# Negated-sine plane, full-row narrow matmuls, a moved radix trick and a new order in an S4 + gated-MLP kernel

## Chip, cores, metric

One core of a Trainium2 chip. The metric is device time in microseconds (us) of one launch. Before the change: 361.38 us, the median of three runs (360.59 to 361.48).

## The reference, cut to what matters

Sequence length L = 2048, width D = 640, state N = 128, MLP width F = 1728, all bf16.

```python
def _A_ref(u, ...):                      # S4: u is the layernorm of x
    logdA = dt * (A_re + 1j * A_im)
    P = exp(logdA[:, :, None] * l)       # table over N and l
    K = einsum("dn,dnl,dn->dl", Cc, P, dB).real
    y = irfft(rfft(pad(u)) * rfft(pad(K)))[:L]
    return y + u * Dskip
h  = x + _A_ref(layernorm(x), ...)
g, up = layernorm(h) @ w_gate, layernorm(h) @ w_up
return h + (sigmoid(g) * up) @ w_down
```

## The kernel before

The kernel K is factored into two tables, A and B, that PE multiplies group by group (`pk`). Picking matmuls gather the lags (`ps_kv`), their spectra are formed (`ps_xk`), and VectorE multiplies them with the spectra of u. The sequence is cut into four blocks of 512 rows; each block b has an inverse transform (`ps_y`), a residual, a LayerNorm and an MLP. Block b's MLP on PE runs beside the spectral products and the inverse of block b + 1.

Table B's steps, one C-tile of 160 columns at a time; the last two lines are the half-size operations:

```python
t   = s * sine_plane(mi)         # both halves (re, im) at once
dst = s * cosine_plane(mi)
V(dst[:, 0], dst[:, 0], t[:, 1], ALU.subtract)
V(dst[:, 1], dst[:, 1], t[:, 0], ALU.add)
```

The narrow matmuls, one contraction row each (cut):

```python
MM(pv[0:32, 0], lhsT=one[64:65, :], rhs=edge[64:65, dc]..., tile_position=(64, 0))          # "one",  32 columns
MM(ps[0:NL, 1, ...], lhsT=last[0:1, q, 0, :], rhs=kv[0:1, 3 + q, ...])                      # "pair", NL = 14 columns
MM(ps[96:128, a, W:2 * W], lhsT=sel[32:33, 0, :], rhs=edge[32:33, ...], tile_position=(32, 96))  # "sel", 32 columns
```

The radix trick for a block in `R4` (12 VectorE operations, half as many inverse matmuls), the transposition of the normalised rows, and the down-projection's residual (cut):

```python
for ft in range(1 if b in R4 else 2): ...        # inverse: 16 or 32 matmuls
# turn(b): DMA if DT[b], else 20 PE transposes, through ml_po's banks if PW, else ml_pg's
po = ... # second half of the down-projection: ml_pg/ml_pu banks if PW, else ml_po's
tb = Wd[:, 15, 320 * c:320 * c + 320]
nc.scalar.copy(tb, po[k][c][:, 0:320])
nc.vector.tensor_tensor(h2[:, c], tb, h2[:, c], ALU.add)
```

The order of instructions comes from a scheduler that reads one priority for each unit of work, in the dictionary `AT`.

Of the kernel before, what the change touches and what calls it, by code (L numbers as in the profile page):

```python
# [8 lines left out]
DT = mybir.dt  # L9
F32, BF16, F16, I32, I16 = DT.float32, DT.bfloat16, DT.float16, DT.int32, DT.int16  # L10
AF = mybir.ActivationFunctionType
ALU = mybir.AluOpType
PSUM = bass.MemoryType.PSUM
PI = math.pi
P = 128
# [7 lines left out]
W = 160  # L23
NC = D // W
UH = 320
EO = (1, 3)
R4 = (2,)
AT = {"eb": -38.3, "ea0": -22.2, "tb0": -12.8, "cb": -5.3, "bb0": 10.0, "st0": -13.2, "ta0": 20.7, "ch0": -25.4, "A0": 1.0, "st1": -127.2,
      "st2": -38.2, "st3": 34.0, "tb1": 45.8, "bb1": 28.9, "n0": -8.7, "ta1": 48.0, "ch1": 54.1, "A1": -23.3, "tb2": 49.0, "bb2": 68.1,
      "ea1": 70.7, "n1": 53.4, "ta2": 71.2, "ch2": 33.5, "A2": 32.8, "tb3": 73.0, "bb3": 75.3, "n2": -7.5, "s0": 66.5, "l0": -14.7,  # L30
      "i0": 94.9, "ta3": -15.7, "ch3": -6.7, "A3": -12.7, "n3": 0.8, "s1": 76.0, "l1": -16.4, "i1": 219.0, "i2": -7.7, "LATER": 49.5,
      "LATER2": 98.7, "EARLY": -11.7, "s2": 58.8, "p0": -14.4, "p1": -3.4, "p2": -13.4, "PW": 1, "w0": 29.5, "w1": -19.5, "w2": 66.8,
      "w3": 82.8, "DT": (0, 0, 0, 0), "NG": (1, 0, 0, 0), "TAIL": -45.1, "NA": (1, 2, 0, 0), "SA": (2, 0, 0, 3),
      "K": (42.3, 65.1, 109.8, 202.7), "F": (-18.0, 64.3, 14.3, 46.5), "G": (2.6, 0.5, 2.3, 0)}

# [7 lines left out]
FIRST = {1: 0, 2: 2, 3: 4}  # L43
M_SHIFT = (0, 1, 2, 8, 9, 10)
B_STEPS = ((1, 2, (0, 1, 1), 2), (2, 4, (0, 2, 1), 1), (4, 8, (0, 4, 1), 0), (8, 12, (0, 4, 1), 3), (12, 16, None, 4),
           (16, 18, (0, 16, 8), 5), (18, 21, (12, 17, 2), 5))


# [5 lines left out]
def host_consts():  # L54
# [38 lines left out]
    for c in range(4):  # L93
        pick[4 * np.arange(32) + c, c, np.arange(32)] = 1.0
    last = np.zeros((P, 3, 4, NL))
    for c in range(4):
        last[c, 0, c, 0:4] = 1.0
        last[c, 1, c, 4:10] = 1.0
        last[c, 2, c, 10:14] = 1.0
    one = np.zeros((P, 32))  # L100
# [7 lines left out]
def bc(ap, shape):  # L108
    return ap.to_broadcast(shape)
# [23 lines left out]
def full_kernel(tc, ins, out):  # L133
# [55 lines left out]
    G = cload(xp, "G", [P, 2, 2, 2, 4, P], tag="G")  # L189
    pick = cload(cp, "pick", [P, 4, 32])  # L190
    last = cload(cp, "last", [P, 3, 4, NL])
    one = cload(cp, "one", [P, 32])
    KM = cload(xp, "KM", [P, 2, 2, 2, NK, P], tag="X")
    sel = cload(cp, "sel", [P, 2, 32])
    cor = cp.tile([P, 40], F32, name="cor")
    xc = cp.tile([P, 40], BF16, name="xc")
    edge = cp.tile([96, D], BF16, name="edge")
    sy.dma_start(edge[64:65, :], ins["A_Dskip"].rearrange("(o d) -> o d", o=1))
    uh = cp.tile([NL, D], BF16, name="uhead")
# [26 lines left out]
    for i in range(2):  # L226
# [3 lines left out]
        nc.vector.scalar_tensor_tensor(fr[:, i, 1], phi, 2.0 ** -19, fr[:, i, 0], ALU.mult, ALU.subtract)  # L230
    mg = tabp.tile([P, 2, P], F16, name="mg")
    ones = tabp.tile([P, 1], F16, name="ones")
    nc.gpsimd.memset(ones[:], 1.0)
    nc.gpsimd.memset(mg[:, 0], MAGIC16 / P)
    nc.gpsimd.memset(mg[:, 1], 0.25 / P)

    def turns(items, o, w):

        ps = ps2.tile([P, 2, 512], F32, name="ps_t", tag="p2")
        m = len(items) // 2  # L240
        for a in range(2):
            MM(ps[:, a, 0:m * w], lhsT=mg[:, 0], rhs=bc(ones[:], [P, m * w]), start=True, stop=False)
            for q in range(m):
                src, dk, oo = items[a * m + q]
                for i in range(2):
                    MM(ps[:, a, q * w:q * w + w], lhsT=dg[:, dk, :], rhs=fr[:, src, i, o + oo:o + oo + w], start=False, stop=(q == m - 1 and i == 1))  # L246
        v = ps[:, :, 0:m * w].bitcast(I16).rearrange("p a (n t) -> p a n t", t=2)[:, :, :, 0]

        def quarter():
            for a in range(2):  # L250
                MM(ps[:, a, 0:m * w], lhsT=mg[:, 1], rhs=bc(ones[:], [P, m * w]), start=False, stop=True, skip_group_check=True)

        return v, quarter
# [5 lines left out]
    rstd = cp.tile([P, 16], F32, name="rstd")  # L259
    st = cp.tile([P, 16, 2, 6], F32, name="ln_st", tag="ln_st")  # L260
    nmr = cp.tile([P, 16], F32, name="nmr")
# [32 lines left out]
    def trig_b(c):  # L294
        M = T["MB", c] = tabp.tile([P, 2, 6, W], BF16, name="tabMB", bufs=2)
        v, quarter = turns([(0, 16, 0), (0, 17, 0), (0, 15, 0), (1, 16, 0), (1, 17, 0), (1, 15, 0)], W * c, W)
        act_fn(TWO(M[:, 1]), v, AF.Sin, scale=SIN_SCALE16)
        quarter()
        act_fn(TWO(M[:, 0]), v, AF.Sin, scale=SIN_SCALE16)

    def bases_b(c):
        M = T["MB", c]
        for ri in range(2):
            V(M[:, ri], EB[:, :, W * c:W * c + W], M[:, ri], ALU.mult)

# [68 lines left out]
    def chain_b(c):  # L374
        X, M = T["B", c], T["MB", c]
        tS = tabp.tile([P, 8 * W], BF16, name="tS")
        for d0, d1, src, mi in B_STEPS:
            n = d1 - d0
            t = tS[:, 0:2 * n * W].rearrange("p (i n w) -> p i n w", i=2, n=n)
            dst = X[:, :, d0:d1, :]  # L380
            if src is None:
                for ri in range(2):
                    s4 = X[:, ri, 0:16, :].rearrange("p (a b) w -> p a b w", a=2)[:, :, 0:2, :]
                    t4, d4 = (v.rearrange("p (a b) w -> p a b w", a=2) for v in (t[:, ri], dst[:, ri]))
                    for o4, pl in ((t4, 1), (d4, 0)):
                        V(o4, s4, bc(M[:, pl:pl + 1, mi:mi + 1, :], [P, 2, 2, W]), ALU.mult)
            else:
                s = X[:, :, slice(*src), :]
                V(t, s, bc(M[:, 1:2, mi:mi + 1, :], [P, 2, n, W]), ALU.mult)
                V(dst, s, bc(M[:, 0:1, mi:mi + 1, :], [P, 2, n, W]), ALU.mult)  # L390
            V(dst[:, 0], dst[:, 0], t[:, 1], ALU.subtract)
            V(dst[:, 1], dst[:, 1], t[:, 0], ALU.add)
# [4 lines left out]
    def ln_stats(st, mv, src, r):  # L397
        for hh in range(2):
            nc.vector.bn_stats(st[:, r, hh, :], src(r)[:, 320 * hh:320 * hh + 320])  # L399
        nc.vector.bn_aggr(mv[:, r, :], st[:, r, :, :].rearrange("p a b -> p (a b)"))  # L400

# [52 lines left out]
    def kmm(c):  # L454
# [16 lines left out]
        def diagonal(g1, kts):  # L471
# [5 lines left out]
            for c4 in range(4):  # L477
                for m in range(4):
                    MM(pv[32 * m:32 * m + 32, :, :, c4], lhsT=pick[:, c4, :], rhs=kj[:, :, :, 4 * m + c4], start=not c4, stop=(m > 0 and c4 == 3), tile_position=(0, 32 * m))  # L479
            MM(pv[0:32, 0], lhsT=one[64:65, :], rhs=edge[64:65, dc].rearrange("p (g c) -> p g c", c=4), start=False, stop=True, tile_position=(64, 0))  # L480
            for c4 in range(4):
                MM(pl[:, :, c4], lhsT=last[:, 2, c4, :], rhs=kts[:, :, 80 + c4], start=not c4, stop=False)
            nc.scalar.copy(kv[:, :, 4 * g1:4 * g1 + 4 * GC], ps[:, 0, 0:20 * GC].rearrange("p (j x) -> p j x", j=5))
            for q in range(2):
                MM(ps[0:NL, 1, 0:4 * GC], lhsT=last[0:1, q, 0, :], rhs=kv[0:1, 3 + q, 4 * g1:4 * g1 + 4 * GC], start=False, stop=(q == 1))
            nc.scalar.copy(edge[0:NL, dc], ps[0:NL, 1, 0:4 * GC])
# [31 lines left out]
    def prod(c, fs):  # L518
# [6 lines left out]
        t2 = prp.tile([P, 2, 2, 2, W], BF16, name="t2", tag="t2", bufs=1)  # L525
        for ft in fs:
            V(t1[:, ft], Z0[:, ft, :, :, o:o + W], S01[:, 0, ft, :, :, o:o + W], ALU.mult)
            V(t2[:, ft], Z0[:, ft, :, :, o:o + W], S01[:, 0, ft, :, ::-1, o:o + W], ALU.mult)
        V(y[:, f, :, 0], t1[:, f, :, 0], t1[:, f, :, 1], ALU.subtract)
# [9 lines left out]
    def inv0(c, fs=((0, 1),), done=None):  # L539
# [6 lines left out]
        for a in range(2):  # L546
            with tc.issue_after(T["mm"]):
                MM(pv[:, a], lhsT=ident[:], rhs=hv[:, a], start=True, stop=False)
            if a:
                MM(ps[96:128, a, W:2 * W], lhsT=sel[32:33, 0, :], rhs=edge[32:33, o:o + W], start=False, stop=False, tile_position=(32, 96))  # L550
        for fg in fs:
# [175 lines left out]
    def edges(psp):  # L727
# [5 lines left out]
        nc.scalar.copy(ct[0:8, :].rearrange("p (q w) -> p q w", q=2), ps[0:8, :, 0:UH])  # L733
        sy.dma_start(dcor[:], ct[0:8, :])
        for b, (t0, t1) in ROWS.items():
            sy.dma_start(xc[16 * FIRST[b]:16 * (FIRST[b] + t1 - t0), :], lanes(x2d[512 * b + 508 + t0:512 * b + 508 + t1, :]))
        sy.dma_start(cor[:], lanes(dcor[:]))
        V(xc[:], xc[:], cor[:], ALU.add)
        sy.dma_start(lanes(dxc[:]), xc[:])
        patch(1)  # L740
# [87 lines left out]
def mlp(tc, sc, xp, yp, cp, hs, st, mv, rstd, nmr, gu, Wd, ident, oh, ln_coef, ln_stats_act, later, edges, products, inverse, load_h, patch):  # L828
# [62 lines left out]
    for b in range(NB):  # L891
# [29 lines left out]
        for lp in (0, 2):  # L921
# [23 lines left out]
            for k in range(2):  # L945
# [3 lines left out]
                for c in range(2):  # L949
                    if b < NB - 1:  # L950
                        tb = Wd[:, 15, 320 * c:320 * c + 320]
                        nc.scalar.copy(tb, po[k][c][:, 0:320])  # L952
# [68 lines left out]
```

## Time and profile before

| | before |
|---|---|
| median, us | 361.38 |
| span of the profiled run | 358.8 |
| PE, VectorE, ScalarE busy | 324.9, 285.4, 245.0 |
| first gate matmul of blocks 0, 1, 2, 3 | 152.48, 206.26, 260.69, 310.71 |
| end of the last down-projection matmul | 355.11 |

In the profile's lines PE is TensorE, DVE is VectorE, ACT is ScalarE, POOL is GpSimd and SP is SyncE; L898 is line 898 of the kernel. The granted clock is the share of its full clock that TensorE was allowed. A handover is the time between two blocks' MLPs, in which the next block's rows are normalised and transposed.

The last two rows are read from the trace, and they are the ruler: they cut the span into five stretches. Where nothing in a stretch was changed, the four after the first repeat from run to run within about 0.1 us. Two things limit the ruler. The first stretch scatters: with every engine's instructions in the same order it came out at 152.48, 152.89 and 153.51 us (the kernel before and two variants of its later part). And a stretch can hold a short time of halved clock, which is not the kernel's doing (see "The handover"). The profile's own lines of this kernel are in the prediction below.

### The profile page before, as it was taken

The page shows a single profiled execution, that of the slowest core. Times are in us where ns is not written, and L with a number is a line of the kernel's source. Part 1 is how long each engine was busy: PE and PEld are TensorE (multiplying, and loading weights), DVE is VectorE, ACT ScalarE, POOL GpSimd, SP SyncE. Part 2 cuts the span into 40 slices and gives each one's busy share as a digit, 9 for nine tenths or more (in the row PEclk, how much of TensorE's full clock was granted, in tenths as well). Part 3 has the DMA queues.
Part 4 walks back from the last instruction along what each step waited for, and adds up shares of the span by engine and source line. Part 5 has one row for each costly group of instructions (what it writes and reads, how often), then busy time and mean ns, then how long its engine had stood idle before and what let it go on. Part 6 is the DMA issues. An engine that isn't in the chain of part 4 may idle for free.

```text
span 358.8 us, 6679 instructions
## 1 busy us (share of the span) xinstructions
PE 324.9 (91%) x2604; PEld 205.7 (57%) x2604; DVE 285.4 (80%) x597; ACT 245.0 (68%) x449; POOL 11.6 (3%) x19
## 2 busy tenths in 40 slices
PE   1598979899999999899999899998699999999995
PEld 1385646777586769744456544455444556644463
DVE  4899999999999979789998999998999931221221
ACT  6999997999899645662767755656655578655500
POOL 1011102000000000100001000001000001000000
PEclk9999999999999999999999999999899999999999
DMA  6990000257007159799400250000030000100011
GB/s 178 337 379 3 16 2 2 83 158 266 13 3 221 75 183 357 177 291 299 184 4 0 74 186 36 2 0 2 1 146 3 0 0 2 55 20 1 0 37 38
DMA packets 29703, 34.37 MB, mean 96 GB/s; under 512 B 16988, under 2 KB 25053, under 8 KB 29416
## 3 DMA queue, kind: packets, MB, share of 16 engines
q1 hardware_dynamic: 29672, 33.95, 29.1%
q8 instruction: 20, 0.33, 0.4%
q14 instruction: 11, 0.09, 0.1%
HBM read 24.72 MB, written 9.21 MB: 95 GB/s over the span
## 4 chain that ended last, share of the span: by engine, by line
PE 41%; DVE 32%; ACT 13%; DMA 7%; issue 3%; SPq 2%; POOL 1%; POOLq 0%; DVEq 0%; ACTq 0%
PE ml_pg L898 8%; PE ml_pu L898 8%; PE ml_po L931 6%; DVE u L684 4%; DVE u L685 4%; PE ps_z L449 3%; PE ps_y L556 3%; PE ps_xk L510 3%; DVE u L687 2%; DVE u L688 2%; PE ps_kv L479 2%; PE pk L468 2%; DVE ln_st L399 2%; ACT zs L450 2%; DMA raw<-in_A_C_re_dram 2%
## 5 line engine op out<-in xcount | busy, mean ns | idle before, releaser
L898 PE MATMUL ml_pg<-lnT,Wg 128*128 128x512 bf16 x260 | 64.8, 379 | 0.7 <-ACT ml_sg L906 0.7
L898 PE MATMUL ml_pu<-lnT,Wu 128*128 128x512 bf16 x260 | 64.9, 379 | 0.5 <-ACT Wd L952 0.4
L931 PE MATMUL ml_po<-Wd,ml_hm 128*128 128x320 bf16 x416 | 59.1, 301 | 0.0
L931 PEld LDWEIGHTS <-ml_hm 128*128 128x128 bf16 x416 | 40.1, 98 | 18.7 <-issue 2.4
L906 ACT ACTIVATE ml_sg<-ml_pg 128x512 bf16<-128x512 f32 x52 | 31.2, 599 | 26.0 <-PE ml_pg L898 14.6
L909 DVE TENSOR_TENSOR ml_hm<-ml_ub,ml_sg 128x512 bf16<-128x512 bf16 x52 | 21.8, 419 | 28.4 <-ACT ml_ub L908 28.4
L908 ACT CAST ml_ub<-ml_pu 128x512 bf16<-128x512 f32 x52 | 30.4, 585 | 20.4 <-PE ml_pu L898 20.2
L898 PEld LDWEIGHTS <-Wu 128*128 128x128 bf16 x260 | 25.4, 98 | 31.5 <-issue 1.0
L898 PEld LDWEIGHTS <-Wg 128*128 128x128 bf16 x260 | 25.4, 98 | 29.2 <-issue 0.9
L449 PE MATMUL ps_z<-u,c_G 128*128 128x320 bf16 x192 | 28.8, 298 | 2.2 <-ACT a_cs L273 0.7
L510 PE MATMUL ps_xk<-kv,c_KM 128*128 128x160 bf16 x320 | 26.6, 232 | 2.4 <-ACT zs L450 1.0
L684 DVE TENSOR_TENSOR u<-Z,S 128x1280 bf16<-128x1280 bf16 x34 | 27.7, 817 | 0.1
L685 DVE TENSOR_TENSOR u<-Z,S 128x1280 bf16<-128x1280 bf16 x34 | 27.7, 816 | 0.0
L246 PE MATMUL ps_t<-fr,c_dg 128*128 128x160 f16 (+1 forms) x180 | 20.0, 240 | 6.1 <-DMA c_dg<-s4c_dg 4.3
L510 PEld LDWEIGHTS <-c_KM 128*128 128x128 bf16 x320 | 23.1, 98 | 4.1 <-issue 3.2
L449 PEld LDWEIGHTS <-c_G 128*128 128x128 bf16 x192 | 18.4, 97 | 10.9 <-issue 3.9
L246 PEld LDWEIGHTS <-c_dg 128*128 128x128 f16 x180 | 14.8, 100 | 13.0 <-issue 4.9
L688 DVE TENSOR_TENSOR u<-u,u 128x1280 bf16<-128x1280 bf16 x23 | 18.8, 817 | 0.0
L687 DVE TENSOR_TENSOR u<-u,u 128x1280 bf16<-128x1280 bf16 x23 | 18.8, 816 | 0.0
L468 PE MATMUL pk<-tabB,tabA 128*128 128x84 bf16 x320 | 16.6, 200 | 2.3 <-ACT kts L469 2.0
L468 PEld LDWEIGHTS <-tabA 128*128 128x128 bf16 x320 | 14.4, 97 | 5.2 <-issue 4.3
L469 ACT CAST kts<-pk 128x420 bf16<-128x420 f32 x32 | 15.6, 543 | 2.5 <-PE pk L468 2.4
(157 smaller groups left out, 549.6 us busy)
## 6 DMA issues: line engine op xcount, KB each, us to landing
dz<-zs SPq DMA_DIRECT2D x12, 320.0 KB, 2.2
c_KM<-s4c_KM SPq DMA_DIRECT2D x1, 2560.0 KB, 12.8
dxk<-xk SPq DMA_DIRECT2D x16, 160.0 KB, 2.4
h<-in_A_u_dram SPq DMA_DIRECT2D x4, 640.0 KB, 3.9
eo<-dz SPq DMA_DIRECT2D x4, 640.0 KB, 4.6
S<-dxk SPq DMA_DIRECT2D x4, 640.0 KB, 7.4
Wg<-in_B_w_gate_dram SPq DMA_DIRECT2D x4, 520.0 KB, 7.9
Wu<-in_B_w_up_dram SPq DMA_DIRECT2D x4, 520.0 KB, 7.7
```

The costliest lines, as they stand in the source:

```text
L246: MM(ps[:, a, q * w:q * w + w], lhsT=dg[:, dk, :], rhs=fr[:, src, i, o + oo:o + oo + w], start=False, stop=(q == m - 1 and i == 1))
L449: MM(ps[:, ri, 0:UH], lhsT=G[:, ft, 0 if b in EO else hf, ri, r, :], rhs=us[b][:, r, o:o + UH], start=(r == rr[0]), stop=(r == rr[-1]))
L468: MM(pk[:, i, :], lhsT=A[:, ri, g].rearrange("p e c -> p (e c)"), rhs=B[:, ri, :, 4 * g:4 * g + 4], start=(ri == 0), stop=(ri == 1))
L510: mm = MM(ps[:, hf, ri * W:ri * W + W], lhsT=KM[:, ft, hf, ri, KI[d] + q, :], rhs=kv[:, j, :], start=(q == 0), stop=(q == len(KD[d]) - 1)).ins
L684: V(t1, z, k[:, :, :, hs_], ALU.mult)
L685: V(t2, z, k[:, :, ::-1, hs_], ALU.mult)
L687: V(s1, s1, t1, ALU.add)
L688: V(s2, s2, t2, ALU.add)
L898: nc.tensor.matmul(ps[:], lhsT=W[:, dc, f0:f0 + 128], rhs=lnT[:, dc].rearrange("p a b -> p (a b)"), start=(dc == 0), stop=(dc == 4))
L906: nc.scalar.activation(sg[:], pg[:], AF.Sigmoid)
L908: nc.scalar.copy(ub[:], pu[:])
L931: nc.tensor.matmul(po[k][c][:, 0:320], lhsT=hm[:, ft, 128 * lr:128 * lr + 128], rhs=Wd[:, ft, 320 * c:320 * c + 320], start=(start and ft ...
```

## The change

Its intent: fewer starts of VectorE operations in table B, narrow matmuls that don't change PE's tiling, a shorter handover between MLP blocks, and an order found anew for all of it. `NA` and `SA` count the rows that ScalarE normalises and takes the statistics of, `DT` marks the blocks with transposes by DMA. The core of the diff, with cuts at "...":

```diff
-R4 = (2,)
+R4 = (3,)
-      ... "PW": 1, ... "DT": (0, 0, 0, 0), ... "NA": (1, 2, 0, 0), "SA": (2, 0, 0, 3), ...
+      ... "PW": 0, ... "DT": (0, 0, 0, 1), ... "NA": (3, 0, 2, 3), "SA": (1, 0, 0, 3), ...   # all priorities are new
 def bases_b(c):
-    for ri in range(2):
-        V(M[:, ri], EB[...], M[:, ri], ALU.mult)
+    V(m, bc(EB[...], [P, 2, 6, W]), m, ALU.mult)
+    nc.scalar.mul(M[:, 0:3], M[:, 6:9], -1.0)
 def chain_b(c):
+    if mi > 2:                                   # four of the seven steps
+        pair = M[:, mi - 3:mi + 4:6, :]...       # (-sine, +sine)
+        V(t, s[:, ::-1], bc(pair, [P, 2, n, W]), ALU.mult)
+        V(dst, dst, t, ALU.add)
+        continue
-MM(pv[0:32, 0], lhsT=one[64:65, :], rhs=edge[64:65, dc]..., tile_position=(64, 0))
+MM(pv[0:32, 0], lhsT=one[0:96, :], rhs=edge[:, dc]..., tile_position=(0, 0))
-MM(ps[0:NL, 1, ...], lhsT=last[0:1, q, 0, :], rhs=kv[0:1, 3 + q, ...])
+MM(ps[0:NL, 1, ...], lhsT=last[:, 4 + q, :], rhs=kv[:, 3 + q, ...])
-MM(ps[96:128, ...], lhsT=sel[32:33, 0, :], rhs=edge[32:33, ...], tile_position=(32, 96))
+MM(ps[96:128, ...], lhsT=sel[0:96, 0, :], rhs=edge[:, ...], tile_position=(0, 96))
-for ft in fs:
-    V(t1[:, ft], Z0[...], S01[...], ALU.mult)
-    V(t2[:, ft], Z0[...], S01[..., ::-1, ...], ALU.mult)
+V(g(t1[:, f]), z, k, ALU.mult)
+V(g(t2[:, f]), z, k[:, :, ::-1], ALU.mult)
-tb = Wd[:, 15, 320 * c:320 * c + 320]
+tb = Wd[:, 14 + k, 320 * c:320 * c + 320]
```

## The prediction

> **What bounds the kernel now.** I read the page first: the busy shares, then the slices, then the chain that ended last.
>
> ```profile
> PE 324.9 (91%) x2604; PEld 205.7 (57%) x2604; DVE 285.4 (80%) x597; ACT 245.0 (68%) x449; POOL 11.6 (3%) x19
> ...
> PE 41%; DVE 32%; ACT 13%; DMA 7%; issue 3%; SPq 2%; POOL 1%; POOLq 0%; DVEq 0%; ACTq 0%
> ```
>
> PE is busy for 91%, yet it carries only 41% of the chain; VectorE carries 32% and ScalarE 13%. So no single engine is the bound, and I asked for the busy time of each engine by stage. The columns are the stretch, its length, then PE, PEld, DVE, ACT and POOL busy (count), granted clock, DMA share, GB/s.
>
> ```profile
> 20.00:50.00 30.00, 25.69 (x197) 18.40 (x197) 30.00 (x75) 29.26 (x46) 3.62 (x3) 1.00 0.23 91
> 50.00:110.00 60.00, 55.69 (x673) 41.95 (x673) 59.01 (x123) 55.41 (x99) 2.48 (x2) 1.00 0.26 85
> 110.00:147.00 37.00, 35.14 (x500) 28.38 (x499) 32.54 (x77) 22.71 (x44) 0.00 (x0) 1.00 0.67 208
> 147.00:250.00 103.00, 98.11 (x597) 54.04 (x595) 98.56 (x192) 64.10 (x122) 3.47 (x3) 1.00 0.33 103
> 250.00:262.00 12.00, 8.99 (x64) 5.75 (x62) 12.00 (x25) 7.85 (x14) 0.00 (x0) 0.86 0.00 1
> 262.00:359.00 97.00, 92.94 (x541) 50.53 (x539) 40.30 (x85) 49.25 (x89) 1.01 (x1) 1.00 0.08 28
> ```
>
> From 20 to 50 us VectorE never rests (tables A and B). From 50 to 110 us three engines are nearly full, and the chain passes back and forth between ScalarE and PE. From 110 to 147 us PE sets the pace (ScalarE 61% busy). From 173 to 248 us the chain runs through VectorE's spectral products while PE does the MLP of blocks 0 and 1. From 250 us on PE is the bound, apart from the LayerNorm handovers between blocks. One of those, the chain of block 1 to 2, in order of time:
>
> ```profile
> 248.50 1.46 POOL rstd L416
> ...
> 251.07 2.53 ACT ln L848 x3
> 253.60 0.64 ACT Wd L952 x2
> ...
> 254.28 1.87 PE ml_pt L863 x16
> 256.14 0.65 PE ml_po L942 x3
> 256.79 4.06 PE ml_po L931 x26
> ```
>
> The 16 transposes wait not for the normalised rows, ready at 253.6, but for a ScalarE copy of a down-projection result (L952) that stands behind them in its queue. The waits put 2.66 us before these transposes and 1.79 us before the same ones of the block before. The clock was 0.86 in this stretch.
>
> **What the Trainium skill says.** (1) "TensorEngine Tiling (Array Packing)", Key Properties: changing the tiling mode, as against the tile, drains the TensorE. The trace agrees. In the timeline of PE:
>
> ```profile
> 121.06 0.21 PE L468 MATMUL pk<-tabB,tabA 128*128 128x84 bf16 x1
> 121.20 0.23 PE L485 MATMUL ps_kv<-kv,c_last 1*14 1x80 bf16 x2
> 121.36 0.55 PE L468 MATMUL pk<-tabB,tabA 128*128 128x84 bf16 x10
> ...
> 119.53 0.20 PE L480 MATMUL ps_kv<-edge,c_one 1*32 1x80 bf16 x1
> ```
>
> The matmul before the pair starts at 121.06, the one after it at 121.36, and a matmul of this size follows another at about 0.047 us. So the pair holds PE for about 0.30 − 0.05 = 0.25 us for 160 columns, where full-height matmuls would take 0.05 to 0.07.
> (2) "VectorE: DVE Perf Modes", The TRN2 errata: an SBUF op costs a fixed 58 cycles (60 ns at 0.96 GHz) plus elements over the mode's factor. The trace agrees in spacing: ops of 640 elements follow each other at 0.40 us, of 1280 at 0.735, so 65 ns fixed plus 1/1.92 ns an element.
> (3) The same table gives ScalarE 224 cycles plus elements at 1.2 GHz: 128x480 is then an estimate of 0.59 us. No such op is in this trace; the formula gives 0.72 for 128x640, and the trace has 0.73 (L405) to 0.91 (L848).
> (4) "DMA: Bandwidth & Descriptors", DMA cost and Latency: about 2.0 us fixed, and transposing DMAs at 261 GB/s. This kernel has none; its plain 160 KB issues land in a median of 2.4 us.
>
> **The change part by part.**
> *Table B, negated sine.* Four of the seven steps of each C-tile do one add of double size where they did a subtract and an add. Over four C-tiles that is 4 x 4 x 2 = 32 half-size ops becoming 16. The elements stay the same, so only the starts are saved: 16 here, 4 from the merged base multiplies and 6 from the merged product multiplies (12 become 6): 26 x 65 ns = 1.7 us of VectorE. It adds four ScalarE multiplies of 128x480 at about 0.65 us (between the page and the 640-element rows): +2.6 us.
> *LayerNorm split.* Rows normalised on ScalarE go from 3 to 8, at 0.85 us each: +4.25 us ScalarE, and 5 x 0.36 = −1.8 us VectorE. One row of statistics goes back from ScalarE (−1.85 us, two passes) to VectorE (+0.85). Together with the multiplies ScalarE gets +5.0 us and VectorE −1.7 − 1.8 + 0.85 = −2.65 us, all before about 105 us.
> *Narrow matmuls.* Measured as above: from the start of the full-height matmul before to the start of the one after, less their normal spacing, L480 holds PE 0.38 us x8 = 2.9, the L485 pairs 0.25 x8 = 2.0 to 2.5, L550 0.26 x4 = 1.05. At 0.05 to 0.07 us each the saving is about 4.2 us of PE; some 2.6 of it falls after 110 us, where PE is the bound, the rest where PE has other waits.
> *The radix trick (four subtracts, four adds, four copies on VectorE, about 4.2 us) moves from block 2's inverse to block 3's.* It halves 32 matmuls, so 16 x 0.136 = 2.2 us of PE. Block 2's inverse runs beside block 1's MLP, before the wait of 241 to 254 us, where PE is not the bound: +2.2 there costs nothing. Block 3's runs in 278 to 293 us, between MLP matmuls with no gap: −2.2 us on the path; VectorE is 42% busy there.
> *Transposes of lnT.* They leave the banks shared with the down-projection, whose residual copy also gets a second buffer. The 2.66 and 1.79 us waits lose their cause. Block 3's 20 transposes become four DMAs; 16 of them hold PE for 1.05 us, and 3.6 + 0.4 us of down-projection stand ready to cover a landing. My estimate is 640 KB at the page's 261 GB/s, 2.5 us, plus 2.0 fixed: 4.5 us against 4.0 of cover plus the lead of the first rows.
> *New order.* Priorities only. It puts the spectra of the first C-tile before block 1's forward matmuls; the listing of PE is otherwise close to the one before, and I give it no gain.
>
> On the path, in us:
> - to 50: VectorE a little shorter, the first multiplies in ScalarE: −0.5
> - 50 to 112: of ScalarE's +5.0, its idle time of about 7 takes most: +1.2
> - 112 to 147: narrow matmuls −2.6, of which I take 1.5, since casts of products still hold PE at times; merged prod ops −0.2
> - block 0 to 1: −1.0 of the 1.79
> - block 1 to 2: −1.8 of the 2.66
> - inverse of block 3: −2.2
> - block 2 to 3: transposes −1.0, late landing +0.7: −0.3
>
> The sum is −6.3, so 355.1. Savings made just ahead of a wait tend to be given to that wait, so I give back 0.7: 355.8 us.
>
> **The rivals.**
> *ScalarE becomes the bound from 50 to 112 us.* For: it is 92% busy there, the casts of products (kts) wait in its queue, and it gets up to 5 us more. Against: part of its work is free to move, and the tuned order was chosen with it. If none of the 5 is absorbed the stage is +3 to +4, and the total about 359.
> *VectorE's products still gate block 2.* Its work from stage three's LayerNorm to the last residual of block 2 is 90.9 us before and 93.0 after, because more products of block 3 stand ahead. For: that chain holds 173 to 248 us. Against: part of this work can be passed over. Then −1.8 and −1.0 vanish: about 358.5.
> *The DMA transposes land late.* For: the page's figure gives no slack. A wait of up to 3 us before block 3's matmuls, at a lower granted clock afterwards: 357 to 359.
> *More than I count.* The order may fill the 3.4 us of PE stalls at 190 to 210, the 7.3 at 240 to 260 and a part of the 33 before 150. Recovering a quarter of these 44 us, the firm parts below included, gives −11: about 350.
>
> **Range and chances.** The firm parts are the narrow matmuls and the inverse (−3.7 to −4.8). The rivals each move the time by +3, the last by −5, and I think one of them likely. So 355.8, range 350.5 to 360.5. Two per cent is 7.2 us, a time below 354.2; that needs the handover waits gone and ScalarE's addition absorbed: 0.31. Slower by 2% needs two rivals at once: 0.02. Within: 0.67.
>
> **What would show it.** Right: the waits before the transposes of blocks 1 and 2 under 1 us; the spacing at the narrow matmuls under 0.1 us; inverse matmuls of block 3 halved, with VectorE's added ops beside them; the stage 110 to 147 at least 1 us shorter. Wrong: ScalarE over 97% busy from 50 to 112 us and that stage longer; a wait of PE for a DMA before block 3's gate matmuls; block 2's handover still released by VectorE products with the same 12 us stretch. A gain above 8 us would mean that the order did most of it, which I can't see from the listing.

## The result, and the profile after

356.6 us, the median of four runs (355.88 to 356.86), against 361.31 for the kernel before in the same rounds: ratio 0.987, interval [0.985, 0.989]. A ratio here is the mean time of one kernel's fast runs over that of the other's fast runs of the same rounds, so it is not quite the ratio of the medians. The prediction was 355.8.

The page of the changed kernel, its busy shares and its chain:

```profile
PE 320.4 (90%) x2584; PEld 204.0 (57%) x2584; DVE 283.3 (80%) x570; ACT 245.9 (69%) x455; POOL 11.4 (3%) x20
...
DVE 28%; PE 18%; issue 14%; ACT 2%; POOL 1%; POOLq 0%; DVEq 0%; ACTq 0%
```

PE does 4.5 us less and VectorE 2.1 us less. The chain is no longer comparable: its shares add up to 63%, because the walk back goes from the last LayerNorm through POOL's queue and books 47 us as "issue". A chain that loses its thread like this says nothing about the stretch it skips. The busy time by stage, in the stretches and columns of the prediction:

```profile
20.00:50.00 30.00, 24.96 (x193) 16.57 (x193) 30.00 (x73) 29.97 (x46) 2.31 (x2) 0.94 0.23 93
50.00:110.00 60.00, 52.76 (x658) 41.39 (x655) 57.78 (x106) 57.47 (x103) 3.72 (x3) 1.00 0.25 79
110.00:147.00 37.00, 34.80 (x503) 28.83 (x502) 32.62 (x73) 23.00 (x46) 0.73 (x1) 1.00 0.71 214
147.00:250.00 103.00, 98.02 (x601) 54.54 (x599) 99.38 (x187) 65.30 (x125) 1.42 (x3) 1.00 0.34 105
250.00:262.00 12.00, 11.25 (x85) 7.40 (x85) 11.10 (x25) 8.41 (x16) 0.87 (x1) 1.00 0.01 2
262.00:359.00 97.00, 89.32 (x503) 47.63 (x501) 39.98 (x89) 45.26 (x86) 1.01 (x1) 0.99 0.11 35
```

ScalarE is fuller from 20 to 110 us, VectorE a little emptier, and the stretch of the second handover is now nearly full of PE work at a granted clock of 1.00. But the ruler says how little of that reached the end. Durations of the five stretches, us:

| | start to gates 0 | 0 to 1 | 1 to 2 | 2 to 3 | 3 to end |
|---|---|---|---|---|---|
| before | 152.48 | 53.78 | 54.43 | 50.02 | 44.40 |
| after | 152.61 | 53.51 | 54.11 | 46.78 | 44.40 |

Of 3.7 us by this ruler, 3.24 lie between the first gate matmul of block 2 and that of block 3. There, from the first gate matmul to the last group of gates (`Wl`), 32.40 us became 30.23: the halved inverse, −2.17. One of its four groups, before and after:

```profile
292.00 1.25 PE L790 MATMUL ps_y<-VR,c_IV 128*128 128x320 bf16 x8
...
289.92 0.71 PE L801 MATMUL ps_y<-VR,c_IV 128*128 128x320 bf16 x4
```

From there to block 3's gates 17.62 became 16.55: the transposes that left PE, −1.07. Everything that the change did in the first 260 us, where most of its code is, left 0.46 us, which is less than the first stretch scatters.

### The profile page after: what moved, and what is told of

The parts are those of the page before. It is cut to its first block, busy times and chain, and to the rows that moved or that the text cites. A ratio compares the mean times of both kernels' runs of the same rounds, so it can differ in the third digit from the quotient of the medians.

```text
span 355.0 us, 6617 instructions
## 1 busy us (share of the span) xinstructions
PE 320.4 (90%) x2584; PEld 204.0 (57%) x2584; DVE 283.3 (80%) x570; ACT 245.9 (69%) x455; POOL 11.4 (3%) x20
## 4 chain that ended last, share of the span: by engine, by line
DVE 28%; PE 18%; issue 14%; ACT 2%; POOL 1%; POOLq 0%; DVEq 0%; ACTq 0%
DVE u L694 5%; PE ml_po L942 5%; DVE u L693 5%; PE ml_pg L909 5%; PE ml_pu L909 4%; DVE u L696 3%; DVE u L697 3%; DVE ml_hm L920 2%; DVE VR L704 2%; PE ps_y L565 1%; DVE Z L673 1%; DVE y L701 1%; DVE y L702 1%; DVE h L805 1%; ACT ln L859 1%
## 5 line engine op out<-in xcount | busy, mean ns | idle before, releaser
L457 PE MATMUL ps_z<-u,c_G 128*128 128x320 bf16 x192 | 30.3, 307 | 4.5 <-ACT zs L458 2.7
```

Of the source, the lines that this page charges most:

```text
L457: MM(ps[:, ri, 0:UH], lhsT=G[:, ft, 0 if b in EO else hf, ri, r, :], rhs=us[b][:, r, o:o + UH], start=(r == rr[0]), stop=(r == rr[-1]))
```

## Experiments

Twelve kernels ran, all with a correct result. "Before" is the kernel before in the same rounds.

| run | median | before | ratio, 95% interval | to gates 0 | 0 to 1 | 1 to 2 | 2 to 3 | 3 to end |
|---|---|---|---|---|---|---|---|---|
| after | 356.60 | 361.31 | 0.987 [0.985, 0.989] | 152.61 | 53.51 | 54.11 | 46.78 | 44.40 |
| b_radix3_dma | 359.05 | 361.30 | 0.9947 [0.9922, 0.9973] | 152.89 | 53.78 | 56.03 | 46.76 | 44.39 |
| a_radix2 | 358.59 | 361.30 | 0.9928 [0.9903, 0.9952] | 152.15 | 53.51 | 52.06 | 50.71 | 44.39 |
| a_peturn3 | 357.93 | 361.30 | 0.9912 [0.9887, 0.9937] | 152.58 | 53.51 | 54.10 | 47.99 | 44.39 |
| a_radix23 | 362.58 | 361.30 | 1.003 [1.0002, 1.0057] | 152.72 | 53.51 | 52.08 | 54.73 | 44.39 |
| a_onerow | 358.32 | 360.27 | 0.9951 [0.992, 0.9981] | 153.63 | 53.52 | 54.10 | 46.78 | 44.39 |
| a_wide | 356.80 | 360.27 | 0.9901 [0.9872, 0.993] | 152.45 | 53.51 | 54.10 | 46.78 | 44.39 |
| a_halves | 359.48 | 360.27 | 0.998 [0.9946, 1.0014] | 155.05 | 53.51 | 54.10 | 46.84 | 44.40 |
| a_nasa | 363.12 | 360.27 | 1.0075 [1.0045, 1.0104] | 158.93 | 53.50 | 54.11 | 46.84 | 44.39 |
| b_handover | 360.90 | 361.14 | 0.998 [0.9952, 1.0008] | 153.51 | 53.91 | 54.71 | 50.17 | 44.39 |
| a_pw1 | 356.87 | 361.14 | 0.9872 [0.9848, 0.9897] | 152.41 | 55.03 | 52.56 | 46.68 | 44.39 |
| a_oldorder | 367.04 | 361.14 | 1.0145 [1.0119, 1.0172] | 163.09 | 53.89 | 54.89 | 46.85 | 44.40 |
| a_best | 359.95 | 361.14 | 0.9957 [0.9937, 0.9977] | 152.76 | 53.73 | 55.54 | 48.19 | 44.39 |

A name that starts with a is the changed kernel with one edit, one with b the kernel before with one edit. The stretches are from the one profiled run of each; they say where a difference lies, the medians how large it is. The runs were made in three calls, each on another chip, in which the kernel before had medians of 361.30, 360.27 and 361.14 us; a difference of medians across calls carries up to about 1 us of that.

### The radix trick and block 3's transposes

`b_radix3_dma`, on the kernel before:

```diff
-R4 = (2,)
+R4 = (3,)
-"DT": (0, 0, 0, 0)
+"DT": (0, 0, 0, 1)
```

> The kernel before with two constants of the change only: radix trick in block 3 in place of block 2, block 3's transposes by DMA. Tail theory (the gain of 4.7 us lies after 260 us: 2.2 from the halved inverse of block 3, 1.05 from its transposes): nearly all of the gain, -3 to -4 us, so about 357.5 to 358.5, first gate matmul of block 2 to that of block 3 46.8 us instead of 50.0. Rival (the new order and the freed handovers gave it): under 1.5 us of gain.

The stretch from block 2 to 3 came out as expected, 46.76. But block 1's stretch grew from 54.43 to 56.03, and the median fell by 2.25 us only, between the two theories. So moving the trick seems to have a price in block 1. This profile isn't a clean measure of it: the granted clock is halved from 246.4 us for 6.8 us (in the kernel before for 3.4 us), and the 52 down-projection matmuls at 247.85 us took 9.88 us, where 7.24 is usual. Three more of its runs, at a mean granted clock of 1.00, had spans of 357.1 to 357.5 us, like this one's 357.3, so much of that loss is hidden in a wait.

`a_radix2`:

```diff
-R4 = (3,)
+R4 = (2,)
```

> The changed kernel with the radix trick put back into block 2. Tail theory: block 2's stretch grows by the 16 matmuls of 0.136 us, +2.2, and block 1's shrinks by at most the 1.5 by which its last gate matmul came later, so between +0.7 and +2.2 us. Rival that I wrote in the prediction (in block 1 the doubled inverse is hidden): +2.2 in full.

+2.0 us by the medians, +1.4 by the ruler, within the range of the tail theory. The parts are larger than that: block 1's stretch is 2.05 shorter, block 2's 3.93 longer. The first has the size of the 16 inverse matmuls, 16 × 0.136 = 2.2: in the 29 us from 207 to 236 PE is busy for 29.00 us in the changed kernel, and it reaches the down-projection 33.48 us after the first gates, in `a_radix2` 31.31. But the order of VectorE changes too: between the first gates and the last residual of block 2 it has 68 operations of spectral products, in the changed kernel 77. Which of the two sets the price isn't separated here, and `a_pw1` below speaks for VectorE. The second is more than 2.2, and the timeline of `a_radix2` shows the rest, a wait of 1.59 us of PE in block 2. The columns are start, length, engine, line, operation, what it writes and reads, size, count, and in brackets the wait and its releaser:

```profile
278.39 0.81 DVE L693 TENSOR_TENSOR u<-Z,S 128x1280 bf16<-128x1280 bf16 x1
...
282.14 0.41 DVE L920 TENSOR_TENSOR ml_hm<-ml_ub,ml_sg 128x512 bf16<-128x512 bf16 x1
282.58 0.60 ACT L917 ACTIVATE ml_sg<-ml_pg 128x512 bf16<-128x512 f32 x1 [2.37 <-DVE ml_hm L920]
283.23 1.24 PE L909 MATMUL ml_pg<-lnT,Wg 128*128 128x512 bf16 x5 [1.59 <-ACT ml_sg L917]
```

Read it from the bottom: the gate matmul waits for a bank that the sigmoid has to empty; the sigmoid waits for its output buffer, which the MLP's multiply has to free; and that multiply stands in VectorE's queue behind block 3's spectral products. With the trick in block 2, PE reaches this place earlier than VectorE can.

`a_radix23`, the trick in both blocks:

```diff
-R4 = (3,)
+R4 = (2, 3)
```

> The changed kernel with the radix trick in blocks 2 and 3 both. If PE's inverse sets the LayerNorm of block 2 (its last gate matmul came 1.5 us later after the change): -1 to -1.5 us. If VectorE's queue sets it (the chain is VectorE from 150 to 250 us), the added 12 operations of about 4.2 us come on that chain: +1 to +4 us.

+6.0 us by the medians, more than the second theory's range. Block 1's stretch is the short one (52.08), block 2's is 54.73: 12 more VectorE operations in the same queue. Its timeline has the same wait, larger:

```profile
284.03 1.44 PE L909 MATMUL ml_pg<-lnT,Wg 128*128 128x512 bf16 x3 [5.04 <-ACT ml_sg L917]
```

The granted clock is halved from 282.8 to 289.6 us, around the end of that wait, so a part of the 7.95 us by which this stretch is longer than the changed kernel's is the clock and not the wait. Up to the end of block 3's products, PE and VectorE are close to a tie: saving PE time beyond that buys a wait.

`a_peturn3`:

```diff
-"DT": (0, 0, 0, 1)
+"DT": (0, 0, 0, 0)
```

> The changed kernel with block 3's lnT transposed on PE again. Tail theory: +1.05 us (20 transposes on the path), plus up to 0.5 if the first ones wait for the copies: +0.8 to +1.6. Rival (the landing of the DMAs is what sets block 3's start, so they gain nothing): within 0.3 us.

+1.33 us by the medians, +1.21 in the one stretch that it touches (47.99 against 46.78). The transposes by DMA gain what they free. The timeline of the changed kernel shows why they are hidden:

```profile
300.02 5.28 SPq L868 DMA_TRANSPOSE lnT<-ln  x4
...
303.47 3.71 PE L942 MATMUL ml_po<-Wd,ml_hm 128*128 128x320 bf16 x26
...
307.01 1.24 PE L909 MATMUL ml_pg<-lnT,Wg 128*128 128x512 bf16 x5
```

The queue is held until 305.30, by each of the four for 1.2 to 1.3 us, and PE has down-projection until it starts the gates at 307.01 without a wait. The profile's page gives 2.6 us from issue to landing, so the last, issued at 304.02, has landed by about 306.6: some 0.4 us to spare.

### The narrow matmuls

`a_onerow` puts back the one-row forms:

```diff
-MM(pv[0:32, 0], lhsT=one[0:96, :], rhs=edge[:, dc]..., tile_position=(0, 0))
+MM(pv[0:32, 0], lhsT=one[64:65, :], rhs=edge[64:65, dc]..., tile_position=(64, 0))
 # likewise the pair (row 0) and sel (row 32, tile_position=(32, 96))
```

> The changed kernel with the three narrow matmuls of one row each again (weights and rows as before). Height theory (a matmul of less than full height drains PE, as I predicted; full-height ones save 4.2 us of PE, 1.5 on the path): first gate matmul of the MLP +1.0 to +2.0 us later. Width theory (the trace of the changed kernel still shows 0.26 us around the full-height pairs of 14 columns and the 96-row ones of 32 columns; only the one among other 32-column matmuls fell from 0.38 to 0.19): 8 x 0.19 = 1.5 us of PE, and +0.2 to +0.8 us on the path.

The first gate matmul comes 1.02 us later and every other stretch is unchanged; the medians differ by 1.5 from `a_wide`. VectorE and ScalarE run in the same order as in the changed kernel, so this is the cost of the rows alone, 1.0 to 1.5 us, with the first stretch's scatter of about 0.5 on it. The size on the path lies between the theories, but the mechanism is the second's. In the timeline of the changed kernel the pair looks as it did before:

```profile
122.17 0.21 PE L476 MATMUL pk<-tabB,tabA 128*128 128x84 bf16 x1
122.31 0.24 PE L493 MATMUL ps_kv<-kv,c_last 128*14 128x80 bf16 x2
122.48 0.55 PE L476 MATMUL pk<-tabB,tabA 128*128 128x84 bf16 x10
```

From 122.17 to 122.48 are 0.31 us, with one row before (0.30 in the prediction) as with 128 now. The numbers before "128x80" are the rows and columns of weights: 128*14. Measured in the same way, sel holds PE 0.26 to 0.27 us in both kernels. Only "one" fell, from 0.38 (0.20 in one of its eight places) to 0.19 us in six of them (0.02 and 0.11 in the other two), and it stands among other matmuls of 32 columns.

`a_wide` tests that directly. It packs the zero-padded weights so that windows of 72 columns exist, and writes 72 PSUM rows of which 14 are read:

```diff
-MM(ps[0:NL, 1, ...], lhsT=last[:, 4 + q, :], rhs=kv[:, 3 + q, ...])
+MM(ps[0:72, 1, ...], lhsT=last[:, NL * q:NL * q + 72], rhs=kv[:, 3 + q, ...])
-MM(pl[:, :, c4], lhsT=last[:, c4, :], ...)                  # pl: 14 rows
+MM(pl[:, :, c4], lhsT=last[:, 28 + NL * c4:100 + NL * c4], ...)   # pl: 72 rows
```

A first version widened the pair alone; it accumulated onto PSUM rows that nothing had written. That is why the four single ones are wide too.

> The changed kernel with the pairs of 14 columns, and the four single ones before them, made 72 columns wide (the added columns are zero or never read). Width theory (it is the number of columns, by which PE's tiling mode is chosen, that drains): the 0.26 us around the pairs that stand among full-size matmuls falls to 0.05-0.12, time -0.3 to -1.2 us. Height theory: nothing changes, within 0.3 us.

The timeline of `a_wide`, at the same place:

```profile
122.24 0.20 PE L474 MATMUL pk<-tabB,tabA 128*128 128x84 bf16 x1
122.27 0.23 PE L491 MATMUL ps_kv<-kv,c_last 128*72 128x80 bf16 x2
122.34 0.54 PE L474 MATMUL pk<-tabB,tabA 128*128 128x84 bf16 x10
```

0.31 us became 0.10. Less the normal spacing, the pair holds PE 0.07 us where it stands among full-size matmuls, as I had predicted for rows. So what drains here is a change in the number of columns, 128 to 14 and back, and the rows matter where the columns already agree. The time did not follow: the step from "one" to the four single ones now changes the width where it hadn't and takes 0.27 in place of 0.19 us, and the first gate matmul came 0.16 us earlier, below what I expected. The width theory holds for the mechanism; as an improvement this edit is within noise, since 0.16 us is less than this stretch scatters.

### Table B and the LayerNorm split

`a_halves` goes back to half-size operations in all steps and drops the ScalarE multiplies:

```diff
-if mi > 2:
+if False:
-nc.scalar.mul(M[:, 0:3], M[:, 6:9], -1.0)
```

> The changed kernel without the negated-sine plane: two half-size operations again in all seven steps, no ScalarE multiplies, order unchanged. By my working VectorE gets 16 starts of 65 ns = +1.0 us and ScalarE -2.6 us. If VectorE bounds up to 50 us and ScalarE has slack: +0.2 to +0.5 us. Rival (ScalarE became the bound from 50 to 110 us, 57.5 of 60 us busy): -0.5 to -1.5 us.

The first gate matmul comes 2.4 us later, outside both expectations. The rival falls as far as its sign goes: ScalarE lost 2.7 us of multiplies and its stage got longer. But this run isn't a clean measurement. Priorities are the same, yet the scheduler orders by them together with when things become ready, and of the 283 VectorE operations of this stretch in the changed kernel, the longest sequence in common order is 241; the LayerNorm of block 2's rows, for one, comes at 67 us and not at 53. How much of the 2.4 is the operations and how much the order stays open.

`a_nasa` restores the LayerNorm split:

```diff
-"NA": (3, 0, 2, 3), "SA": (1, 0, 0, 3)
+"NA": (1, 2, 0, 0), "SA": (2, 0, 0, 3)
```

> The changed kernel with the split of LayerNorm's rows between VectorE and ScalarE as before (three rows normalised on ScalarE in place of eight, five rows of statistics in place of four). ScalarE -2.4 us, VectorE +1.0. If ScalarE is what held the first stage at 152.6 us: -0.5 to -2 us. If the two engines are in balance, as the annealed order suggests: within 0.7 us either way.

+6.3 us before the first gate matmul, against both. The same caution holds: 243 of 283 in common order, and the clock is halved twice in this stretch, at 53.3 and 90.8 us. `a_oldorder` keeps the changed code and its constants and takes the priorities of before:

```diff
-AT = {"eb": -25.6, "ea0": -43.2, "tb0": -16.9, ...
+AT = {"eb": -38.3, "ea0": -22.2, "tb0": -12.8, ...   # PW, DT, NA and SA as in the changed kernel
```

> The changed kernel with the priorities of before; the code, the constants for the radix trick, the transposes, the banks and the LayerNorm split stay. If the code makes the gain: within 1.5 us of the changed kernel. If code and order fit only each other (the split of before under the new order cost 6 us): +3 to +8 us, all of it before the MLP starts.

+10.5 us to the first gate matmul, more than expected, and about 1 us in the two stretches after it, the second of which holds a halved clock. In its stretch from 20 to 50 us PE is busy for 15.96 us of 30, where the changed kernel has 24.96. So in the first 150 us code and order fit each other only as a pair. An undo of one of them overstates its worth, and no sum of such undos gives the change.

### The handover

`b_handover`:

```diff
-"PW": 1
+"PW": 0
-tb = Wd[:, 15, 320 * c:320 * c + 320]
+tb = Wd[:, 14 + k, 320 * c:320 * c + 320]
```

> The kernel before with only the handover's part of the change: transposes through the gate's banks, second half of the down-projection through its own banks, residual copies in two buffers. Theory (the waits of 1.79 and 2.66 us before the transposes came from those shared banks and the single buffer): -1.5 to -3 us, most of it between the last gate matmul of block 1 and the first of block 2 (23.6 us before, 21.7 after). Rival (the LayerNorm chain of VectorE, POOL and ScalarE sets the handover anyway, since the changed kernel's block 0 to 1 gained only 0.3 us): within 0.7 us.

No gain is seen: ratio 0.998 with an interval that holds 1 and reaches from −1.7 to +0.3 us. None of its stretches is shorter than before by more than 0.01, but here the ruler proves little: the profiled run is the slowest of the six (362.29), and 1.03 of its length lies in the first stretch, where no instruction changed. `a_pw1` undoes the banks in the changed kernel:

```diff
-"PW": 0
+"PW": 1
```

> The changed kernel with the transposes and the second half of the down-projection in the old banks again, two buffers kept. If the banks are the cause of the waits: block 0 to 1 +0.5 to +1.5 us, block 1 to 2 +1.5 to +2.5, in all +1.5 to +3.5. If the single buffer was the cause: within 0.7 us.

+0.27 us by the medians. The waits came back as expected, the time did not. The waits of PE for transposes in `a_pw1`:

```profile
200.90 1.05 PE L874 MATMUL ml_pt<-c_ident,ln 128*128 128x128 bf16 x16 [2.38 <-ACT Wd L963]
255.10 1.05 PE L874 MATMUL ml_pt<-c_ident,ln 128*128 128x128 bf16 x16 [2.35 <-ACT Wd L963]
```

and those of the changed kernel around its second handover, between 244 and 256 us:

```profile
244.56 0.31 PE L953 MATMUL ml_po<-Wd,ml_hm 64*128 64x320 bf16 x1 [1.26 <-DVE ml_hm L931]
...
249.97 3.69 PE L942 MATMUL ml_po<-Wd,ml_hm 128*128 128x320 bf16 x26 [0.87 <-ACT Wd L963]
...
254.58 0.45 PE L881 MATMUL ml_pt<-c_ident,ln 128*128 128x128 bf16 x5 [0.58 <-ACT ln L859]
...
255.68 0.38 PE L881 MATMUL ml_pt<-c_ident,ln 128*128 128x128 bf16 x4 [0.17 <-ACT lnT L883]
```

One wait of 2.35 became five (a fifth, of 0.15, is left out here): 3.03 us. Over both handovers the waits listed in the timeline add up to 4.73 us in `a_pw1` and 4.62 in the changed kernel; on the kernel before, 6.16 without the edit and 5.20 with it, and that 1 us doesn't show in its stretches. The rival of my expectation holds: PE has a fixed amount of down-projection to put beside the LayerNorm chain, and where it pauses is free to move.

In the ruler, `a_pw1` loses 1.52 in the first handover's stretch and wins 1.55 in the second's. The trace says why. The loss is no matter of banks: the granted clock (0.50, behind the five engines) is halved for 3.4 us, and 26 matmuls took 5.34 us that took 3.71 in the second handover:

```profile
202.20:205.60 3.40, 3.40 (x15) 1.94 (x14) 3.40 (x6) 2.81 (x5) 0.00 (x0) 0.50 0.65 190
...
202.26 5.34 PE L942 MATMUL ml_po<-Wd,ml_hm 128*128 128x320 bf16 x26
...
256.46 3.71 PE L942 MATMUL ml_po<-Wd,ml_hm 128*128 128x320 bf16 x26
```

So PE comes to block 2's handover 1.32 us later than in the changed kernel (down-projection from 240.92 and from 239.60). Yet the last addition of block 2's residual, with which its LayerNorm chain starts, doesn't move. The changed kernel, `a_pw1` and `a_radix2`:

```profile
243.15 0.49 DVE L805 TENSOR_TENSOR h<-Wd,h 128x640 bf16<-128x640 bf16 x1
...
243.06 0.48 DVE L805 TENSOR_TENSOR h<-Wd,h 128x640 bf16<-128x640 bf16 x1
...
240.22 0.48 DVE L805 TENSOR_TENSOR h<-Wd,h 128x640 bf16<-128x640 bf16 x1
```

From there to block 2's gates are 17.08 us in the changed kernel and 16.94 in `a_pw1`. VectorE is busy for 26.91 of the 27 us from 222 to 249 in both. So in the changed kernel VectorE's queue, and not PE, sets when block 2 starts, and 1.3 us of PE's time vanished in its waits.

A second thing shows in the busy times of the stretch from 250 to 264 us; the figure after the five engines is the granted clock. `b_handover`:

```profile
250.00:264.00 14.00, 12.82 (x85) 8.21 (x84) 12.73 (x26) 8.70 (x16) 1.11 (x1) 0.88 0.01 2
```

The changed kernel, the same stretch:

```profile
250.00:264.00 14.00, 13.25 (x94) 8.33 (x94) 13.10 (x29) 9.43 (x18) 0.87 (x1) 1.00 0.01 2
```

After the pauses the clock drops in one and not in the other: in `b_handover` the 24 down-projection matmuls after the transposes took 4.58 us, in the changed kernel the same 24 took 3.42. The Trainium skill, "TensorE: Matmul & The Clock Gate", Part 1, says that an idle window of about 3.4 us halves PE's clock and that these windows run freely, so the moment is a matter of phase. The traces agree with the size (1.2 us lost here). They don't show the window before it as idle: in the 3.41 us before the drop PE was busy for 0.47 us in the kernel before, 1.32 in `a_pw1` and 2.23 in `b_handover`. They agree with the chance: the changed kernel and `a_wide` have no such drop in the second handover, the kernel before has one. There the 16 transposes took 1.87 us (1.05 in `a_pw1`) and the next 26 matmuls 4.13 (3.69 in the changed kernel); from these transposes to the gates were 6.41 us, in `a_pw1` 4.90, so about 1.5 us in all. So the second handover's −0.32 contains a clock drop that the profiled run of the changed kernel happened not to have there.

The record has the mean granted clock of every run, though not where it fell. The 33 runs of the kernel before had a median span of 357.8 us at 1.00, 359.2 at 0.993 to 0.995 and 360.4 at 0.989 to 0.991, so by this estimate a window of halved clock costs it about 1.3 us. The changed kernel's four runs, earlier and all at 0.993 to 0.995, have 354.9: at the same clock it is still 4.3 us shorter, so the drops don't make the gain.

### A try to beat both

`a_best` joins the wide pairs with transposes by DMA in blocks 1 and 2 as well:

```diff
-"DT": (0, 0, 0, 1)
+"DT": (0, 1, 1, 1)
 # and the edit of a_wide
```

> A try to beat both: the changed kernel with the 72-column pairs, and with the transposes of blocks 1 and 2 by DMA as well as block 3's. In block 3 the four DMAs end 5.3 us after their first issue and before the gate matmuls need them; in blocks 1 and 2 the rows are normalised at 200 and 254 us and the gates start at 206 and 260, so the slack is about 0.5 us. If they land in that time: -1.0 us for each of the two blocks and -0.2 for the pairs, 354.4 to 356. If they share the queue with loads and land 2 us later: +1 to +3 us.

It is 3.35 us slower than the changed kernel by the medians. In the first of the two handovers the landing is late:

```profile
206.49 1.25 PE L907 MATMUL ml_pg<-lnT,Wg 128*128 128x512 bf16 x5 [1.18 <-DMA lnT<-ln]
```

What was hidden in block 3 is not hidden in block 1. The larger losses, 1.43 and 1.41 us, are in the next two stretches. In the trace the first holds a halved clock (52 matmuls in 8.91 us, usually 7.24) and gates that start at 262.03, with the last of their four DMAs landed at 261.94, and the second a wait of PE for VectorE of 1.19 us before an inverse. The best kernel is the changed one; `a_wide` can't be told from it.

## Why the prediction was right, and which of its steps were not

The time, 356.6, lies in the range and 0.8 us above the forecast, and within 2% was the likeliest class. By its own steps, the measured figure from the ruler:

| step | forecast | measured | verdict |
|---|---|---|---|
| to 50 us | −0.5 | first `pk` matmul 50.74 to 49.67 | size off, −1.1 |
| ScalarE, 50 to 112 | +1.2 | last table A cosine on ScalarE 102.7 to 104.0: +1.3 in all, so +2.4 in this stage | mechanism consistent, size off |
| narrow matmuls | −1.5 | −1.0 (ruler), −1.5 (medians) by `a_onerow` | mechanism wrong for two of the three |
| to first gates, sum | −1.0 | +0.13 | no gain beyond the scatter |
| block 0 to 1 | −1.0 | −0.27 | wrong: the banks gain nothing |
| block 1 to 2 | −1.8 | −0.32 | wrong for the same reason, and it left out the trick's price; 1.5 us of clock drop before |
| inverse of block 3 | −2.2 | −2.17 | right |
| block 2 to 3 | −0.3 | −1.07 | the DMAs landed in time |
| sum | −6.3, taken as −5.6 | −3.7 (ruler), −4.7 (medians) | |

The steps, one by one:

**Narrow matmuls.** "full-height matmuls would take 0.05 to 0.07" failed for two of the three. I read the Trainium skill's "Changing tiling mode ... drains" (TensorEngine Tiling, Key Properties) and took the one row for the mode. The page lists the modes by rows and columns, and the columns were what I overlooked. The widened pair (0.31 to 0.10 us) shows it. Of the 4.2 us of PE that I counted, "one" gave 2.88 − 1.28 = 1.6, measured before and after around its eight places; the rest did not come.

**The handovers.** "The 2.66 and 1.79 us waits lose their cause" was true and worth nothing. Under rivals I had a queue of VectorE that still gates block 2, with more products of block 3 ahead, and that one came true: from the first gates to the last residual of block 2 are 88.92 us before and 90.54 after, with 70 and then 77 operations of spectral products in between, and `a_pw1` shows that PE's own lateness doesn't matter there. The trace of the kernel before also held a step that I did not take: the waits between the last gates and the next could be added up, and what would remain of them without the banks could be asked. Both directions of the experiment show no gain, within about 1.7 us.

**The radix trick.** "+2.2 there costs nothing" failed: block 1's stretch pays 2.05 (`a_radix2`; `a_radix23`, which has no clock drop there, agrees). I placed the inverse "before the wait of 241 to 254 us" and overlooked that a wait for a chain begins when the chain does: the last residual of block 2, with which the LayerNorm chain starts, comes later (its last addition ended at 241.88 before and 243.64 after). Whether the longer inverse delays it, or the VectorE order that goes with it, stays open. Block 3's −2.2 was right, and a_radix2 shows a second gain that I had not seen, the 1.59 us for which PE would have waited on VectorE in block 2. On the kernel before, which has no such wait, the two constants together gave 2.25 us by the medians and 1.25 by the ruler, of which the transposes are about 1.1.

**ScalarE.** I priced a normalised row at 0.85 us, from other lines of that size. The very line that the change moves, L432, took a mean of 1.02 in the kernel before and 0.975 after (L440).

**Block 2 to 3.** I booked +0.7 for late landings. There was no wait for a DMA, and the step gained the 1.07 us that the 16 transposes hold PE.

**The order.** I gave it nothing. It can't be given a number: the code without the order is 10.5 us worse in the first stage. What can be said is that code and order together left the first 152 us as they were, within their scatter.

**The signs.** Of the signs of being right, the waits before the transposes (0.17 to 0.58 us) and the halved inverse showed, and from table A's last cosine to the gates are 1.2 us less (49.76 to 48.56); the spacing at the narrow matmuls stayed above 0.1 us. Of the signs of being wrong, ScalarE's 97% and the wait for a DMA did not show; block 2's handover does still hang on VectorE.

So the forecast was near the mark because errors of both signs cancelled: too much gain for the banks and the narrow matmuls and a price of the radix trick left out, against too little for the DMAs, the first 50 us, and the 0.7 that I gave back. What is shown as the gain is block 2's stretch, 3.24 of 3.7 us. The 1 us between ruler and medians is mostly the choice of profiled runs: the one of the kernel before took 360.56 us, 0.75 below the median, the changed one's 356.76, 0.16 above it.

## What to carry to other kernels

Cut a long kernel at a few events that every version has, and compare the stretches: that separates parts that a median of the whole blends, and it shows at once where nothing changed. Before booking a wait as a gain, add up all waits of the engine between the two events that a dependent chain ties together; if the chain stays, a freed wait reappears next door. And work that is moved "beside a wait" is free only if it doesn't move the start of the chain that is waited for: ask which engine's queue sets that start (here VectorE's). Before comparing one stretch of two profiles, look in both for a time of halved clock.

## What the Trainium skill lacked or had wrong

- "TensorEngine Tiling (Array Packing)", Key Properties: it gives the drain no cost. Here a pair of 14 weight columns among full-size matmuls held PE 0.26 us with 1 row and with 128; with 72 columns 0.07. A 32-column matmul with 1 row among 32-column ones of 128 rows held it 0.38, with 96 rows mostly 0.19.
- "DMA: Bandwidth & Descriptors", Anatomy of one DMA (the fixed cost, stated for the GpSimd path) and Latency (the rate of transposes): the estimate from them for four transposes of 160 KB in a row was 4.5 us. From SyncE they held their queue 5.28 us, 1.2 to 1.3 each, and the last landed 6.6 us after the first was issued; that the queue takes them one by one is what decides how many fit into a gap.
- "VectorE: DVE Perf Modes", the ScalarE row of the errata table: 128x480 from SBUF to SBUF is 0.59 us by the formula; the four new multiplies took a mean of 0.673, and the row normalisations of 128x640 (L440) took 0.975 against 0.72, while another operation of that size (L413) took 0.73.
